# Attention and two expert layers on one core: another order table, and P's halves with the rotated q/k tile in a pool of their own

## The chip, the cores and the metric

The kernel runs on one core of one Trainium2 chip. The metric is the time of one execution on the device in microseconds; lower is better. The core has TensorE (PE in the rows; PEld are its weight loads), VectorE (DVE), ScalarE (ACT), GpSimd (POOL) and SyncE (SP), which here issues the DMAs.

## The reference

```python
q, k = rotate(q), rotate(k)            # [4, 8, 576, 64]: half-split RoPE, angles from the position
attn = softmax(q @ k.T / 8) @ v        # each of 32 heads over 576 positions
x = attn.transpose(0, 2, 1, 3).reshape(2304, 512)
h = x @ w_in                           # [512, 2048]
x = (h * clip(h + 3, 0, 6) / 6) @ w_out
h = x @ w_in2
P = a[0] + a[1] * h + a[2] * h**2 + a[3] * h**3
Q = 1 + abs(b[0]) * abs(h) + abs(b[1]) * h**2
y = (P / (Q + 1e-6)) @ w_out2
```

q, k, v and the weights are random; the weights reach the kernel as 64-bit numbers, and their upper bits are decoded to 32-bit floats on the chip.

## The kernel before

Nearly every product is made from fp16 halves: a 32-bit operand becomes a high half (a rounded copy) and a low half (what the copy lost), and three matmuls take high by high, high by low and low by high.

**Weights.** Each weight matrix comes as 16 raw tiles of 512 KB (`load_raw`). `decode` turns one into floats with two steps on ScalarE (L422, L424) and one on VectorE (L427); `bound` takes the sum of its squares on ScalarE (L442, written into a tile `junk` that nobody reads), `total` adds such sums over the partitions with a small matmul (L453), and from that comes the scale with which `split16` (L432 to L434) makes the halves. For the first layer's w_out, a VectorE maximum over all 16 bounds (L486, tile `wao`) stands before the first of its 16 splits.

**Attention.** `start_qk` loads q and k of a pair of heads (L613, L616); `prep_qk` rotates them. The tile `ropea` first holds the turned halves (L640), then, for the same bytes, the fp16 halves of the rotated q and k, from which a DMA transpose makes `qkt` (L675, L679). For pairs 1 and 3 the buffer `gh` stands in for `ropea`. `unit` handles a block of 128 or 64 query rows of two heads: S = q kT on TensorE (L704, L707; L711 and L715 for the last key block), the row maximum on VectorE (L719) with its scaling on one of three engines (L725, L727), exp on ScalarE (L736). In the first eight units, the wide ones, P is transposed by TensorE (L751), copied to `pt` (the helper `copy`: L311 on ScalarE, L315 or L317 on VectorE, L313 on GpSimd), and multiplied by V in 32-bit floats (L785). In the others a tile `p16` (two buffers) gets P's high half by the helper and its low half from a subtraction (L758); one DMA transpose (L761) brings both to `pt`, and PV follows (L794). `norm` divides by the row sums (L812 to L824, L842); DMA transposes bring the output to layer 1's layout.

**First layer.** `layer1` works on 256 tokens at a time: x times w_in (L899), the relu (L906, L908), gh by the helper, gl by a subtraction (L912), times w_out (L927). The result goes to DRAM through `y1d` (L939).

**Second layer.** Its weights are decoded and split while the first runs (`load_w2`, `split_w2` at L1043 and L1053). `w2am`, the bound of its w_out, gives scales that the chain needs. `layer2` computes hidden columns (L1151, to `hx` and `hh` in PSUM), the ratio P/Q in a chain of ScalarE and VectorE steps over tiles lq, ls, lt, lr (L1177 to L1193; the raw tiles and y stand in for them at first), and the second product (L1203). Results leave by the helper and L1217.

**What sets the order.** The code does not issue instructions as it runs. Each step is recorded in a `Plan` with the engines it may use. At the end `order()` decodes the table `ORDER`: each number names an operation (x // 12), its engine (a letter of "PADGQN"), and a PSUM bank (x % 2), and the operations are issued in that sequence:

```python
o, e = self.ops[x // 12], "PADGQN"[x % 12 // 2]
...
res = pl.order()
for o, e in res:
    o.fn(e)
```

So the table sets the order on every engine and every choice among engines. A tile gets its place in the memory at its first use in that sequence (`Til.__call__`), as the next bytes of its pool; the pools `const`, `attn` and `right` lie on the two sides of SBUF. When attention ends, `swap` frees the pools of its side for layer 2.

Of the kernel before, what the change touches and what calls it, by code (L numbers as in the profile page):

```python
# [23 lines left out]
H = 8  # L24
# [76 lines left out]
    'PXqjv<`X4ky{$}|ZO2xVXBfA<gSM{FUX01S>FBr3Z<t@8aVTWFAo&~2MWrs-^)r<WD>Io5xu48rbQtsK(3vsh0_$2%o2BE*7jip<@q9~W9^LY^',
    'LWxz$W|fo~%|v7!7RZcNYK{ms5QM6P!G=5qF#G1<hheBqmw6gJy=LL@=?`M6!2;|D=G&f1HUXgo?vc~wK6b8Vx|9&~(;aqE4O<cUu@#e}iTj=%',
    'L_;Y%X*va=kEYlNJW7XQ($g)UIo7d1lo|2O*cSqo9}dGKyG446+5MjUM`_&}dSgAgAqC;CwIhdM$FCpMS(~_eC>>)48$guZ&l#}%aGQ-CkN#p9',
    '&!%I1>gB=U$j@5*W4LEUV3w^OL>b_DXW=vK^MR>@+bo3WDX|KGX9nJEiN6T+#dYX2NAv1nKHeTUb1?6Z9`wQ(>xFu=1K&B`>Y$Hlp9sMZ_C81M',
    'vr^3U*O+L95YLllgX~B2&k#RMu;b9fc5|vQCOSMeLvNnJNb2z3hxu^*c-}7xJ(tZbsl^V%bJ+)<3YNw@OdZCRyO{ZD#E}kn^ZMyUw8qyvAC0|H',
# [1204 lines left out]
```

## Time and profile before

| what | us |
|---|---|
| median of 3 runs | 1074.39 |
| lowest and highest | 1069.35, 1077.87 |
| span of the profiled execution | 1067.9 |
| its own time beside the span | not given |
| TensorE busy | 971.1 |
| VectorE busy | 908.9 |
| ScalarE busy | 738.2 |
| GpSimd busy | 186.2 |

The span is what the profiler recorded of one execution, from the first instruction to the last; the runs' times are measured around the whole. The granted clock of TensorE is 1.00 when the chip lets it run at 2.4 GHz throughout a stretch, less where part of it ran at 1.2 GHz.

### The profile page before, as it was taken

How to read it: one execution, taken by the hardware profiler on the slowest of the kernel's cores; microseconds unless marked ns; L12 is line 12 of the kernel's file. 1: busy time of each engine (PE TensorE's matmuls, PEld its weight loads, DVE VectorE, ACT ScalarE, POOL GpSimd, SP SyncE). 2: the span in 40 equal slices, each digit the busy share in tenths (PEclk: the TensorE clock that was granted, in tenths of full speed). 3: DMA queues.
4: the chain of work that ended last, by engine and by line, in shares of the span. 5: the costliest groups of instructions: out<-in, count | busy, mean ns of one | idle time of the engine just before them, and what ended most of it. 6: DMA issues, size and time to landing. Idle time of an engine off the chain costs nothing.

```text
span 1067.9 us, 20042 instructions
## 1 busy us (share of the span) xinstructions
PE 971.1 (91%) x7978; PEld 686.2 (64%) x7978; DVE 908.9 (85%) x1389; ACT 738.2 (69%) x1144; POOL 186.2 (17%) x165
## 2 busy tenths in 40 slices
...
GB/s 263 251 223 200 93 120 130 171 152 154 139 162 169 157 147 141 164 106 150 145 80 207 235 165 115 21 40 0 40 41 40 1 39 2 11 1 50 1 20 40
DMA packets 253853, 117.04 MB, mean 110 GB/s; under 512 B 223552, under 2 KB 241088, under 8 KB 253760
## 3 DMA queue, kind: packets, MB, share of 16 engines
...
## 4 chain that ended last, share of the span: by engine, by line
PE 41%; DVE 15%; ACT 7%; issue 3%; POOL 1%; ACTq 0%; DVEq 0%; POOLq 0%
PE h L927 10%; PE ac L1203 10%; PE h L899 8%; PE hx L1151 4%; PE hh L1151 4%; PE h L794 3%; DVE lt L1183 2%; PE s L704 1%; DVE lt L1184 1%; DVE lq L1188 1%; DVE lt L1189 1%; DVE lt L1191 1%; DVE lgl L1193 1%; ACT ls L1178 1%; ACT lq L1177 1%
## 5 line engine op out<-in xcount | busy, mean ns | idle before, releaser
L899 PE MATMUL h<-xt,w 128*128 128x256 f16 x1728 | 199.2, 274 | 5.4 <-DVE t L908 2.8
L927 PE MATMUL h<-gh,w 128*128 128x256 f16 x1080 | 189.1, 273 | 0.0
L899 PEld LDWEIGHTS <-w 128*128 128x128 f16 x1728 | 168.6, 99 | 26.6 <-issue 6.5
L927 PEld LDWEIGHTS <-w 128*128 128x128 f16 x1620 | 156.6, 98 | 18.3
L1203 PE MATMUL ac<-w2o,lgh 128*128 128x512 f16 x516 | 153.4, 379 | 0.5 <-ACT lgh L1192 0.5
L1151 PEld LDWEIGHTS <-w2i 128*128 128x128 f16 x900 | 87.8, 98 | 98.5 <-issue 7.9
L927 PE MATMUL h<-gl,w 128*128 128x256 f16 x540 | 147.2, 273 | 0.0
L736 ACT ACTIVATE e<-s,mx,qal 128x576 f32<-128x576 f32 (+1 forms) x144 | 115.7, 831 | 14.8 <-POOL mx L727 6.1
L719 DVE TENSOR_REDUCE mx<-s 128x2 f32<-128x1152 f32 (+1 forms) x80 | 99.0, 1242 | 5.7 <-PE s L707 4.8
L1151 PE MATMUL hh<-x,w2i 128*128 128x512 f16 (+1 forms) x468 | 100.3, 359 | 2.8 <-DVE y1m L1083 1.4
L1203 PE MATMUL ac<-w2o,lgl 128*128 128x512 f16 x258 | 97.8, 379 | 1.1 <-DVE lgl L1193 1.1
L1151 PE MATMUL hx<-x,w2i 128*128 128x512 f16 (+1 forms) x432 | 91.0, 357 | 6.3 <-DVE lt L1184 3.3
L1203 PEld LDWEIGHTS <-lgh 128*128 128x128 f16 x544 | 53.1, 98 | 64.0 <-issue 1.2
L906 ACT ACTIVATE t<-h,half,d 128x512 f32<-128x512 f32 (+1 forms) x96 | 61.5, 667 | 43.1 <-PE h L899 33.1
L758 DVE TENSOR_TENSOR p<-e,p 128x1152 f16<-128x1152 f32 (+1 forms) x63 | 79.8, 1267 | 7.2 <-ACT p L311 6.1
L794 PE MATMUL h<-v,pt 128*128 128x130 f16 (+3 forms) x1440 | 75.5, 207 | 8.9 <-DVE t L908 3.2
L794 PEld LDWEIGHTS <-pt 128*128 128x128 f16 (+1 forms) x1440 | 71.7, 100 | 14.1 <-issue 13.0
L704 PE MATMUL s<-qkt 64*128 64x512 f16 (+2 forms) x576 | 57.6, 327 | 8.2 <-DMA qkt<-ropea 5.3
L908 DVE SCALAR_TENSOR_TENSOR t<-t,h 128x512 f32<-128x512 f32 x72 | 48.9, 679 | 16.1 <-ACT t L906 16.0
L311 ACT ACTIVATE p<-e 128x1152 f16<-128x1152 f32 (+1 forms) x53 | 58.0, 1093 | 3.0 <-DMA pt<-p 1.4
L424 ACT ACTIVATE raw<-raw,down 128x512 int32<-128x512 uint16 x64 | 48.1, 758 | 14.1 <-DMA raw<-in_moe_w_in_dram 11.4
L1181 DVE SCALAR_TENSOR_TENSOR lq<-ls,kc,lq 128x1024 f32<-128x1024 f32 (+1 forms) x38 | 44.3, 1168 | 12.8 <-ACT lq L1177 9.4
...
## 6 DMA issues: line engine op xcount, KB each, us to landing
...
```

The lines of the kernel that those rows point to most:

```text
L311: act.activation(out, in_, AF.Copy, scale=scale)
L704: pe.matmul(s()[:, a:b], lhsT=kq(1, y, 64 * h, 64 * h + 64)[:, cc * 128:cc * 128 + 128], rhs=kq(0, z, 64 * h, 64 * h + 64)[:, c:c + b - a] ...
L719: op("D", c_dve(n), lambda e: vec.reduce_max(mx()[:, 0, 0:g], sv().rearrange("p (g n) -> p g n", g=g), axis=AX.X, negate=True), r=[s], w=[ ...
L736: act.activation(et()[:, h * (n // g):(h + 1) * (n // g)], sv()[:, h * (n // g):(h + 1) * (n // g)], AF.Exp, bias=mx()[:, 1, h:h + 1], sca ...
L758: op(EN("lo"), c_sub(n), lambda e: EL[e].tensor_tensor(ph()[:, n:2 * n], et()[:, 0:n], ph()[:, 0:n], ALU.subtract), r=es + [(ph, 0)], w=[( ...
L794: pe.matmul(ob()[r0:r0 + m, o:o + k], lhsT=w, rhs=vv[:, 0:k], start=(z == 0 and j == 0), stop=(z == 1 and j == 4))
L899: pe.matmul(hp()[:, o:o + NQ], lhsT=wt[kk]()[:, z, c:c + 128], rhs=x, start=(n == 0), stop=(n == 11))
L906: act.activation(seg(t, c, n), seg(hp, c, n), AF.Relu, bias=half(), scale=x()[:, g:g + 1])
L908: op("D", c_dve(2 * NQ), lambda e, t=t, hp=hp: vec.scalar_tensor_tensor(t(), t(), two(-15), hp()[:, 0:2 * NQ], ALU.min, ALU.mult), r=[hp], ...
L927: pe.matmul(yp()[:, o:o + NQ], lhsT=w[:, s_, m_ * 128:(m_ + 1) * 128], rhs=gt()[:, f], start=(f == 0 and z == 0), stop=(f == KF - 1 and z ...
L1151: pe.matmul(hp()[:, x * n:x * n + n], lhsT=wi[kk]()[:, z, c:c + 128], rhs=xt()[:, kk, y, 0:n], start=(i == 0), stop=(i == 11))
L1203: pe.matmul(accs[j][i]()[0:m], lhsT=g(gt)[:, y * n + x:y * n + x + m], rhs=wt, start=(f == 0 and z == 0), stop=(f == KF - 1 and z == 2))
```

## The change

The table is replaced. The operations are the same, and in the built program TensorE has 15,529 instructions before and after, SP 381 and 381; of the operations that may run on more than one engine, many change the engine (VectorE 1391 to 1390 instructions, ScalarE 1048 to 1047, GpSimd 170 to 172). Beside the table, `junk` becomes 832 bytes wide, and `ropea` and `p16` move from the pool `attn` to a new pool `even` ahead of it, with p16 allocated first. In the built programs p16's two buffers lie at bytes 105,984 and 110,592 of each partition before and at 18,432 and 23,040 after; ropea lies at 50,944 and then at 27,648.

```diff
 ORDER = (
-    'c-lo+4NP3wbw2m~&6_umnK8>c6BfCI5K3J{kxLxpP95qZLMU>OMcomllu+UzmpW)m9cmGauBd|?>Jp2k1R<BY6N_$;LtR9Xi!5XjLR@OiTErz5',
...
+    'c-l>PePC48weQ;JoH=vm%$W}Y4k5)DVw#H)5hEh<cwC#NNK+akr7=btX+SO)H6rptF3%fdN)cm>NYj|6h!|*$DNQlbh>@m|Vv3Xo5)rwGQA3Pr49U!yGc)',
...
-    junk = const.tile([128, 10 * D], mybir.dt.uint8, tag="junk", name="junk")
+    junk = const.tile([128, 832], mybir.dt.uint8, tag="junk", name="junk")
+    pool_of("even", "attn")
     pool_of("attn", "attn")
...
-        tbt = tl("right", [128, KF, NQ], F16, "gh") if far else tl("attn", [128, 4, NS, D], F32, "ropea", PR["rp"])
+        tbt = tl("right", [128, KF, NQ], F16, "gh") if far else tl("even", [128, 4, NS, D], F32, "ropea", PR["rp"])
...
-            ph = tl("attn", [128, 4 * S], F16, "p16", PR["p16"])
+            ph = tl("even", [128, 4 * S], F16, "p16", PR["p16"])
...
-    left = swap(("attn", "psa"), "attn", to_left)
+    left = swap(("attn", "even", "psa"), "attn", to_left)
...
     res = pl.order()
+    for tag in ("p16", "ropea"):
+        pl.tags["even", tag][0]()
     for o, e in res:
         o.fn(e)
```

In the changed kernel the lines stand four further down (L736 is L740, L758 is L762; the helper's L311 is L314).

SyncE at the start of the program, before. `raw` are weight tiles, `nat` the q and k of a pair of heads, `tab` the rotation's tables:

```order
L410 DMA raw<-in_moe_w_in_dram 128x1024 x2
L360 DMA tab<-in_tables_dram 128x640
L547 DMA vnat_106<-in_v_dram 128x2x256
L549 DMA vnat_106<-in_v_dram 64x64 x2
L410 DMA raw<-in_moe_w_in_dram 128x1024 x2
L613 DMA nat_130<-in_k_dram 128x2x256
L616 DMA nat_130<-in_k_dram 64x64 x2
L410 DMA raw<-in_moe_w_in_dram 128x1024
L613 DMA nat_130<-in_q_dram 128x2x256
```

and after:

```order
L414 DMA raw<-in_moe_w_in_dram 128x1024
L617 DMA nat_101<-in_k_dram 128x2x256
L620 DMA nat_101<-in_k_dram 64x64 x2
L364 DMA tab<-in_tables_dram 128x640
L617 DMA nat_101<-in_q_dram 128x2x256
L620 DMA nat_101<-in_q_dram 64x64 x2
L414 DMA raw<-in_moe_w_in_dram 128x1024 x2
L617 DMA nat_125<-in_q_dram 128x2x256
L620 DMA nat_125<-in_q_dram 64x64 x2
```

The first k stands second in the queue and its q fifth; before, four raw tiles, the tables and a v stood ahead of k.

ScalarE where the last wide units run, before. `junk,wao` is the bound of a tile of w_out, `w_..<-raw` and `raw<-raw` its decoding, `e` an exp, `pt` a copy of the transposed P:

```order
L311 ACTIVATE pt<-s 128x1152
L442 ACTIVATE junk,qam<-nat_130 128x640
L736 ACTIVATE e,es<-s,mx,qal 128x576
L422 ACTIVATE w_13_970<-raw 128x512
L424 ACTIVATE raw<-raw,down 128x512 x2
L422 ACTIVATE w_14_983<-raw 128x512
L442 ACTIVATE junk,wao<-w_12_942 128x512
L422 ACTIVATE f_986<-raw 128x512
L424 ACTIVATE raw<-raw,down 128x512
L442 ACTIVATE junk,wao<-w_13_970 128x512
L442 ACTIVATE junk,wao<-w_14_983 128x512
L442 ACTIVATE junk,wao<-f_986 128x512
```

and after, up to the last wide unit:

```order
L314 ACTIVATE w_10_818<-w_10_469,wps 128x512
L740 ACTIVATE e,es<-s,mx,qal 128x576 x2
L446 ACTIVATE junk,wao<-w_1_754 128x512
L446 ACTIVATE junk,wao<-w_2_803 128x512
L314 ACTIVATE w_12_861<-w_12_537,wps 128x512
L314 ACTIVATE w_15_870<-w_0_678,wps 128x512
L314 ACTIVATE pt<-s 128x1152
L426 ACTIVATE w_0_889<-raw 128x512
L740 ACTIVATE e,es<-s,mx,qal 128x576 x2
L314 ACTIVATE xu_459<-h_78 128x2x64
L446 ACTIVATE junk,wao<-w_0_889 128x512
L314 ACTIVATE xu_604<-h_79 128x2x64
```

Before, the sixteen tiles of w_out are decoded and bounded around the last wide exps, up to the bound on the last line; after, three of the bounds stand there, the others follow among the later units, and copies of P and of the split w_in (`wps`) have taken their places.

VectorE where layer 2 begins, before. `w2o` are splits of the second w_out, `raw` and `y` are buffers in which the P/Q chain works at first:

```order
L1181 SCALAR_TENSOR_TENSOR raw_9298<-raw_9302,kc,raw_9298 128x1024
L1183 TENSOR_TENSOR raw_9300<-raw_9300,hh 128x1024
L1184 SCALAR_TENSOR_TENSOR raw_9300<-raw_9300,cg,hh 128x1024
L1053 SCALAR_TENSOR_TENSOR w2o_9317<-w2o_8704,w2qs,w2o_9317 128x512
L1189 SCALAR_TENSOR_TENSOR raw_9300<-raw_9300,cg,raw_9302 128x1024
L1188 SCALAR_TENSOR_TENSOR raw_9298<-raw_9298,raw_9302 128x1024
L1053 SCALAR_TENSOR_TENSOR w2o_9322<-w2o_8684,w2qs,w2o_9322 128x512
L1191 SCALAR_TENSOR_TENSOR raw_9300<-raw_9298,raw_9300 128x1024
L1053 SCALAR_TENSOR_TENSOR w2o_9327<-w2o_8806,w2qs,w2o_9327 128x512
L317 TENSOR_SCALAR w2o_9330<-w2o_8814,w2qs 128x512
L1193 TENSOR_TENSOR y_9236<-raw_9300,y_9236 128x1024
```

and after (L1185 and L1187 are the former L1181 and L1183, and so on):

```order
L1185 SCALAR_TENSOR_TENSOR raw_9178<-raw_9211,kc,raw_9178 128x1024
L1187 TENSOR_TENSOR raw_9194<-raw_9194,hh 128x1024
L1057 SCALAR_TENSOR_TENSOR w2o_9226<-w2o_8326,w2qs,w2o_9226 128x512
L1188 SCALAR_TENSOR_TENSOR raw_9194<-raw_9194,cg,hh 128x1024
L1057 SCALAR_TENSOR_TENSOR w2o_9258<-w2o_8360,w2qs,w2o_9258 128x512
L1192 SCALAR_TENSOR_TENSOR raw_9178<-raw_9178,raw_9211 128x1024
L1193 SCALAR_TENSOR_TENSOR raw_9194<-raw_9194,cg,raw_9211 128x1024
L1057 SCALAR_TENSOR_TENSOR w2o_9280<-w2o_8380,w2qs,w2o_9280 128x512
L1195 SCALAR_TENSOR_TENSOR raw_9194<-raw_9178,raw_9194 128x1024
L1057 SCALAR_TENSOR_TENSOR w2o_9304<-w2o_8412,w2qs,w2o_9304 128x512
L1197 TENSOR_TENSOR y_9159<-raw_9194,y_9159 128x1024
```

Before, some splits stand in a row with their helper copies (L317); after, one split stands between nearly every two steps of the chain.

## Rows read from the trace of the kernel before

**Rows 1.** The page: span, and busy time of each engine.
```profile
span 1067.9 us, 20042 instructions
PE 971.1 (91%) x7978; PEld 686.2 (64%) x7978; DVE 908.9 (85%) x1389; ACT 738.2 (69%) x1144; POOL 186.2 (17%) x165
```

**Rows 2.** Four stages: length, busy us by engine, granted clock, DMA share, GB/s.
```profile
0.00:126.30 126.30, 65.48 (x426) 55.65 (x427) 106.14 (x225) 108.75 (x232) 17.98 (x23) 0.89 0.73 209
126.30:180.00 53.70, 51.06 (x554) 43.34 (x552) 51.85 (x75) 37.93 (x62) 13.91 (x13) 0.96 0.61 120
180.00:500.00 320.00, 311.01 (x3536) 265.00 (x3535) 296.32 (x464) 215.28 (x344) 87.62 (x72) 1.00 0.70 152
...
625.00:725.00 100.00, 89.36 (x592) 57.15 (x589) 84.04 (x127) 74.13 (x126) 28.36 (x25) 1.00 0.19 64
```

**Rows 3.** TensorE's timeline at the first L899 and the first L927.
```profile
126.32 4.62 PE L899 MATMUL h<-xt,w 128*128 128x256 f16 x24
...
162.91 0.27 PE L927 MATMUL h<-gh,w_s 128*128 128x256 f16 x1
...
165.53 0.66 PE L794 MATMUL h<-v,pt 128*128 128x130 f16 x11
```

**Rows 4.** TensorE by line, 0 to 126.3 us: busy, mean | idle, releasers.
```profile
L453 PE MATMUL h<-wam,ones 128*128 128x1 f32 x32 | 8.2, 355 | 27.0 <-DVE ones L362 15.0 <-ACT junk L442 11.6 <-DVE qpi L395 0.3
```

**Rows 5.** ScalarE by line, 0 to 121 us.
```profile
L424 ACT ACTIVATE raw<-raw,down 128x512 int32<-128x512 uint16 x32 | 23.8, 753 | 1.7 <-DMA raw<-in_moe_w_in_dram 1.7
L422 ACT ACTIVATE w<-raw 128x512 f32<-128x512 f32 x31 | 20.2, 657 | 7.5 <-DMA raw<-in_moe_w_in_dram 4.9 <-DMA raw<-in_moe_w_out_dram 2.7
L442 ACT ACTIVATE junk<-w 128x512 uint8<-128x512 f32 x31 | 19.4, 625 | 4.5 <-DVE w L427 4.2
...
L311 ACT ACTIVATE pt<-s 128x1152 f32<-128x1152 f32 x3 | 3.3, 1112 | 0.0
```

**Rows 6.** VectorE by line, 0 to 121 us.
```profile
L427 DVE SCALAR_TENSOR_TENSOR w<-w,raw 128x512 int32<-128x512 int32 x31 | 23.3, 754 | 10.8 <-ACT raw L424 9.8 <-ACT w L422 1.0
...
L315 DVE COPY pt<-s 128x1152 f32<-128x1152 f32 x5 | 6.8, 1355 | 2.7 <-PE s L751 2.7
```

**Rows 7.** ScalarE by line and shape, whole span.
```profile
L311 ACT ACTIVATE p<-e 128x1152 f16<-128x1152 f32 x45 | 52.1, 1159 | 2.1 <-DMA pt<-p 1.4
```

**Rows 8.** VectorE by line and shape, whole span.
```profile
L758 DVE TENSOR_TENSOR p<-e,p 128x1152 f16<-128x1152 f32 x51 | 69.8, 1368 | 3.7 <-ACT p L311 3.3
...
L912 DVE TENSOR_TENSOR gl<-t,gh 128x512 f16<-128x512 f32 x58 | 43.3, 753 | 3.1 <-POOL gh L313 1.7 <-ACT gh L311 1.4
...
L315 DVE CAST p<-e 128x1152 f16<-128x1152 f32 x7 | 6.2, 892 | 0.7 <-ACT e L736 0.6
```

**Rows 9.** GpSimd by line and shape, whole span.
```profile
L912 POOL TENSOR_TENSOR gl<-t,gh 128x512 f16<-128x512 f32 x14 | 19.2, 1370 | 39.7 <-ACT gh L311 26.2 <-DVE r L842 8.8 <-ACT w2i L422 3.2
...
L758 POOL TENSOR_TENSOR p<-e,p 128x1152 f16<-128x1152 f32 x5 | 11.9, 2373 | 35.3 <-DVE p L315 18.4 <-ACT p L311 12.0 <-DMA nat<-in_q_dram 4.9
...
L313 POOL TENSOR_SCALAR p<-e 128x1152 f16<-128x1152 f32 x4 | 6.8, 1697 | 26.1 <-ACT e L736 10.2 <-DMA pt<-p 8.0 <-DVE r L842 7.9
```

**Rows 10.** Tile p: count: shortest/median/longest ns, first and last start.
```profile
L761 SPq DMA_TRANSPOSE pt<-p x72: 1252/1925/3498, 124.9 to 548.7; - x72
...
L315 DVE CAST p<-e x10: 485/753/1707, 136.4 to 544.0; 128x1152 f16<-128x1152 f32 x7, 128x640 f16<-128x640 f32 x3
```

**Rows 11.** TensorE's timeline, 674 to 730 us: [idle before <-releaser].
```profile
681.92 0.39 PE L1203 MATMUL ac<-w2i,y 128*128 128x512 f16 x1 [0.90 <-DVE y L1193]
...
704.19 2.75 PE L1151 MATMUL hh<-x,w2i 128*128 128x512 f16 x12 [1.34 <-ACT lq L1177]
...
717.60 0.39 PE L1203 MATMUL ac<-w2o,lgl 128*128 128x512 f16 x1 [1.05 <-DVE lgl L1193]
...
725.25 4.92 PE L1151 MATMUL hx<-x,w2i 128*128 128x512 f16 x22 [2.72 <-DVE lt L1184]
```

**Rows 12.** Tile qkt: transposes from ropea, shortest/median/longest ns.
```profile
L679 SPq DMA_TRANSPOSE qkt<-ropea x13: 2511/2642/3946, 61.6 to 464.4; - x13
```

More of the change, by code (lines that the diff above doesn't have):

```diff
@@ L101 @@
[L101 to L105, printed above, removed]
@@ new lines @@
+    'm_f65SGJvTn^(f%qu|6Rd5_~1=-?ULzriUT%)MaVJ8Pe(1Zo9C3XX!=M>P(Z~%YB#{K}R@dRi>v$+d0a5L;;vlU>ykZrAlI$_k2X@*c??-cH~Y+;PH*h?S',
+    '}4gO<mFLYxaa6+xMO=z}ih4I7_?ziP#@k%Vk`SxD2-lu7quoy~ZE?$qj9h2LJm$6H(kJZVgkx9N&o*y5^R;$zB6U(qWNGTVGCNqaSO8Vt)EQgLrfnSIZ;c',
+    'M12Lb`lB(goXvNqXF#rq2s)o(VM{i(F&0(z?w*TP^VKj1-Zg>!-db_pen)_$Bh)k;&^j#&Ya9oy$<jgjsf-?{<7GQHlSK*AWHs?7jSywfy@2@Z!YOY<+B(',
+    'Cl%DlDD?3sJ#E4G)K1*1uEw3NY;!H_bgl6mP3$-1z?45d62#&}7pPKWq{cU-?uH)xgu6kWMNWk03X8pyv=Y{+*{+cFl&>e=MN<fc5}0tr?~t*pbPQL(5D8',
@@ new lines @@
+    'I+iQa;$(=QhUl<`@fUV2(x>B~3vx>pCn(*v;ydpBEiwKo4d1Jmmh{Zd|Vgo<P{U2!$!8k^lQK8(Y&=l*lbotZd=>ml27KG7e#0Q&R_xE6aowKg&mYfpWc+',
+    '^DXk;*6zES;QN>{i~kY+anze*V>q5&AQ>Rs(D++{mNE*cRa-PI$YZ4^g_5;FP3)4=E_UrdRmV&6-kX{b8+{izcR8D$`W7G>(hj<hHywafUUuy(G*#a6><l',
+    'p%-Dpy3?||;@gdKVcseOGB)QqDQu3X`_!i-ewe0p?7mMQ;a2fPT6VQj%@r4YvD?ZV#jyHJT#s_dpkfN2?&zM&)Erw_D2f_ktLddaodOV)yUuK<wkRXr+<`',
+    'rQ`E%kM&vS+@q0ESf!hf($v3Bl+PmcWqG4ad|5W?!Cg917JpmFsM9<zaoa%C|c*-ygCf{0(+qLRC%?N=wv5(Cd@1LtPH*VF;&uTh(DUONLaOXz`W7fST<)',
@@ new lines @@
+    'V@|px>{i=-i`BQKLF`E6`9F{3NsDyJUlD2XwZT2+`>r%|DpBYkGA6`3jlU;k<u3aj*Xc+>;OE9C0%wgTGW=(ppWF8*RtE0IPF$~2Uz_<fzQT`3B~NxDU0S',
+    '8r`kypD6I;W%Fy`l+Bbwp;Eiof$0W~c7RpGFCjy@jUAU(@hYDq3HoOLZaCvhy$W4CEt?qhs|cGf*4-y3_0Kdxo^4;jDWi?kP%2e?)|V1Tbp=Ts$7EIyL>w',
+    'R_p*S@(s+y*^j8B4z8fmXwoLDfEh`Cl)COq9^<-TzQk9yBF$<u6sR^8+~i$&nCUfr`C=73HLU6l2a#|W^U0JX;-|1)@N8IWNO-s(9{_vKl-x!Q*8H7{ZsY',
+    '5VO;Mk{`wvEo++%+THINJpsXI(XZ|VrGkw-fbMlb;hf4b7>+b*1Z}Q!v?uTagxTk(<t<oKBa7$37uToA%>)dmd2Dtn+gj$^uvU{Ry=0LQ;4-=KwZAjb}t#',
@@ new lines @@
+    'rTV`h%1+vCZ8Ax3~t?N_T}nX9A?{sLKbgC4#f3H>O<Vx`-4B>H3Tqoj1LF_F-J`&+oZ+2wOZ86H8|fP2TDLSeIsU*KT%S)l+9)A$O<`36t*kq7MmvZ%X{U',
+    'n68(5JMdTGM}&>uBif_VcccFZq&X^gdw4@Yh)eQTa_jWNt|R74@*!Mcoi-)qaq1!cMyb1o&v)9@eAgDYipTU$QPxs}+O&4VQ`7sy=Wnnl_ClwizzwngC3n',
+    'FRrzzzpU!F5J2g?ElpErA7Htz8LkM?^{uiZ>~=)=Y}>=ic&Z7eTnxY#Ij_hCYx;T3He(u`F1yZSsg%&ZKz#y-NA<-ypyV#x5rE$}k>)99DWpbU=Ujo^oyV',
+    'VAp9_rtinEVjjcfj_TpcQ@(JO3x))#jE5d?t$1<soyycz5G5@;NIAu<yJeNTkR|ornQKuz#?N@)UW||=+CE>OmA_XBp=gldL|r_KALfSQie)0M51;O{zJb',
```

106 lines of the change are left out of this document (49 added, 57 removed).

## Prediction

> **What bounds the kernel now.** I read the busy shares first [rows 1]: TensorE works 971.1 of 1067.9 us. A new order of the same matmuls can give back at most the other 96.8. The busy times by stage [rows 2] say where they lie (length of the stage less PE's busy time): 60.8 us before the first matmul of layer 1 at 126.32 [rows 3], 2.6 up to 180 us, 9.0 in the 320 us of attention and layers mixed, 10.6 in the passage to the second expert layer (625 to 725), 13.8 in all the rest. So the first stage and the passage can gain, and the middle has more to lose than to win.
>
> In the first stage VectorE and ScalarE are hardly idle: DVE 106.1 of 126.3 us, ACT 108.7 [rows 2]. The totals of the bounds (L453) are what TensorE waits longest for: 27.0 us, 15.0 for the first constant and 11.6 for ACT's bounds [rows 4]. Much of both engines' time is the decoding of weights: on ACT 32 L424, 31 L422 and 31 L442 come to 23.8 + 20.2 + 19.4 = 63.4 us [rows 5], on DVE 31 L427 to 23.3 [rows 6]. About half of it is the first layer's w_out, which TensorE first reads at 162.91 [rows 3].
>
> **The prologue.** SP now loads one raw weight tile and then pair 0's k and q; before, two raw tiles, the tables, v and two raw tiles stood ahead of k. Up to its 16th exp ACT has 10 decodes less (19 raw tiles instead of 29). Each is an L424, an L422 and an L442, 0.753 + 0.657 + 0.625 = 2.04 us [rows 5], together -20.4; in their place come 4 copies of the transposed P (4 x 1.112 = +4.4 [rows 5]) and smaller pieces, about +8.5. Added up by the means of all rows the 16th exp stands behind 92.7 us of ACT work, 7.5 less than before. DVE has up to the fourth normalization of attention output 10 decodes less (10 x 0.754 = -7.5), 5 copies of P less (5 x 1.355 = -6.8 [rows 6]) and -4.5 of small pieces: -18.8 us.
>
> But the w_out work is moved, not removed. Counted the same way, the maximum over its 16 bounds (L486) stands behind 114.6 us of DVE work before and 131.0 now, the eighth of its splits (L434) behind 144.4 and 151.4, the sixteenth behind 166.7 and 166.3, the eighth normalization behind 180.9 and 177.0. TensorE does one S, two S of the last key block and three PV more ahead of its first L927, some 5.7 us, so it needs the splits that much later. On ACT the eighth relu of layer 1 (L906) stands behind 159.0 instead of 146.2, 12.8 later. By DVE's later mark the prologue gives 3.9 us, by ACT's early one 7.5; I take **-6**, between them. The ends are -19 (DVE's early lead is kept) and +7 (ACT's 12.8 less TensorE's own 5.7).
>
> **The middle.** Counted in the order, P's hi copies of 1152 columns go from 45, 7 and 4 on ACT, DVE and POOL to 25, 18 and 13; the lo subtractions (L758) from 51 and 5 on DVE and POOL to 43 and 13; layer 1's gl (L912) from 58 and 14 to 46 and 26. By the means of their rows that is on ACT -20 x 1.159 = -23.2 [rows 7], on DVE +11 x 0.892 - 8 x 1.368 - 12 x 0.753 = -10.2 [rows 8], on POOL +9 x 1.697 + 8 x 2.373 + 12 x 1.370 = +50.7 [rows 9]. POOL gives up 21.5 us of other copies and ACT gets some; over all rows that change engine the sums are ACT -6, DVE -17, POOL +29. TensorE is idle for 9.0 of 320 us there, with DVE 92.6% busy (296.3 of 320 [rows 2]), so what DVE sheds buys little: I take **0**. The ends are -9 (all that PE waits) and +8, from this: the same cast of P on DVE took 485 to 1707 ns [rows 10], so something stretches it. If each of the 21 added POOL subtractions held DVE for 1.707 - 0.892 = 0.8 us, DVE would get its 17 back; if DVE stood for all of POOL's added 29 it would have 12 us more than before, where PE has 9.0 us of slack to lose and DVE 23.7; I count two thirds of the 12.
>
> The Trainium skill, SBUF — State Buffer, section "Who interferes with whom", says that VectorE and GpSimd share a pair of ports under an exclusive lock, and so speaks against this part of the change: every subtraction that POOL gets would stand in DVE's way. The 485 to 1707 ns of the cast [rows 10] fit that. By the rule alone the middle stands at its +8 and the sum at 1070; I leave it at 0 because before, with 5 + 14 such subtractions on POOL, PE waited only 9.0 us in the stage.
>
> **The passage.** PE's four longest waits between 674 and 730 us are 0.90, 1.34, 1.05 and 2.72 us, 6.0 together [rows 11], for y, lq, lgl and lt: the chain of P/Q on ACT and DVE, which shares them with the last splits of the second w_out. The new order puts 84 more L927 between the total of that weight's bound, from which layer 2's scales come, and the first L1203: 144 and 24 L1151, before 60 and 24. An L927 takes 0.109 us (24 of them from 162.91 to 165.53 [rows 3]), so the chain gets 84 x 0.109 = 9.2 us more cover; and the splits stand singly between its steps, with 5 slow copies on POOL in place of 8. I take **-6**; the ends are -10 (all idle time of the stage) and 0 (DVE is 84.0 of 100 us busy there [rows 2], and the chain may just be late by other steps of its own).
>
> **The buffers.** The two p16 buffers lie at bytes 105,984 and 110,592 of a partition before, both multiples of 512 as it happens, and at 18,432 and 23,040 now. Only ropea moves, from 50,944 (256 past a multiple) to 27,648. So P's 72 transposes, 1925 ns in the median [rows 10], are not touched: **0**. ropea's 13 took 2511 to 3946 [rows 12]; their queue could win or lose 13 x 1.4 us at the most, work that runs beside 320 us of matmuls but for the first pair, one transpose on the path: -1.4 to +1.4, within the prologue's ends.
>
> **Sum.** The profile gives a span, 1067.9 [rows 1], and no time of the execution beside it; I take the median of the runs for it, 1074.4, with 6.5 us around the span. 1067.9 - 6 + 0 - 6 + 0 = 1055.9 in the span, 1062.4 with the 6.5: **1062 us**.
>
> **Rivals.** (1) Larger gain. DVE's lead of 18.8 is kept because the deferred splits fit into idle time of DVE, 20.2 us in the first stage [rows 2], and the passage gives its 6: 1074.4 - 24.8 = 1050. For it: TensorE is idle 60.8 us there and the second exp stands behind 25.8 us of ACT work, before 48.1. Against: ACT is 86% busy and ends up later. (2) No change, by POOL. Prologue and passage give their 12, and in the middle DVE stands for POOL's added 29 us less its own 17, +12: 1074. For it: the cast's 1707 [rows 10] and DVE's 92.6%. Against: DVE has 23.7 us free there, so part of the 12 is hidden. It decides where DVE's share from 180 to 500 us passes PE's 97%. The skill's port rule above is this rival. (3) No change, by the start. DVE sets the pace from 0 to 180 us (158 of 180 busy [rows 2]) and is only 3.9 ahead at its later mark, and the passage gains nothing: 1070. (4) Slower: w_out late. The first L927 needs the L486 maximum, the scale and the splits. ACT's last bound stands behind 144.4 us of its work, before 107.0, and its last split behind 167.7, before 148.9. If ACT sets the pace there, TensorE stands 12.8 to 18.8 us longer before its first L927s, 15.8 in the middle, and with the passage's -6 the time is 1084. It decides when ACT is busier than DVE between 100 us and the first L927. For it: ACT led in the first stage (108.7 to 106.1). Against: ACT is at 37.9 of 53.7 from 126 to 180 [rows 2] and can catch up. (5) The second half of the change does nothing, as p16 was aligned; my sum has it so, and only if P's transposes depend on ropea's place would it differ.
>
> **How the numbers follow.** A measurement of this kernel can tell about 1%, 10.7 us, from no change: faster is below 1063.6, slower above 1085.1. The forecast, with 1055 to 1069 as its own range, has 0.42, of which 0.26 lies below 1063.6. Rival 1 has 0.20, rival 2 0.12, rival 3 0.12, rival 4 0.14, of which 0.09 lies above 1085, as with the passage's gain lost it would be 1090. Faster is 0.26 + 0.20 = 0.46; slower is 0.09 and 0.04 for rival 2 with neither prologue nor passage gained (1074.4 + 12 = 1086), 0.13; the same is the remaining 0.41. The range for 8 in 10 goes from 1046, under rival 1 by the 4 more that the passage could give, to 1081, the larger part of rivals 2 to 4 but the w_out case at its full price.
>
> **What would show it.** The prologue: the first L899 at 107 to 120 us and the first L927 before 163; a wait of PE at L927 for the splits (w of L434 or L311) of over 3 us is rival 4. The middle: DVE below 296 us from 180 to 500 and L758's mean at 1368 show no lock, both higher is rival 2. The passage: PE idle under 5 us from 625 to 725, with waits for lq, lt, y and lgl under 1 us each. The buffers: P's transposes within 5% of 1925; if they fall by a tenth or more, my reading of the buffers was wrong. A span with PE idle for over 97 us makes the forecast wrong as a whole.

## The result, and the profile after

| | before | after |
|---|---|---|
| median, us | 1074.76 (8 runs, 1069.35 to 1077.87) | 1082.19 (8 runs, 1079.36 to 1086.13) |
| span of the profiled execution, us | 1067.9 | 1081.2 |
| first L899 / first L927 / last PV, us | 126.3 / 162.9 / 558.0 | 120.2 / 178.1 / 577.7 |

The changed kernel takes 1.0097 times as long as before, with a 95% interval of 1.0074 to 1.0120: slower by just under 1%, some 10 us by the ratio (the two medians of the table are 7.4 us apart), where 12 us less were forecast. In the profiled executions of the changed kernel and of e1 to e13 the time is 1.7 to 1.9 us above the span, so before's span of 1067.9 belongs to an execution of about 1070 (an estimate), one of its fastest; the two spans differ by more than the times do. In all rows of the changed kernel a line stands four further down (L903 is L899, L931 is L927, L762 is L758).

The page of the changed kernel, span and busy times; [rows 1] are its counterpart:

```profile
span 1081.2 us, 20075 instructions
PE 988.2 (91%) x7978; PEld 698.9 (65%) x7978; DVE 901.0 (83%) x1388; ACT 732.7 (68%) x1143; POOL 194.3 (18%) x167
```

TensorE is busy for 17.1 us longer with the same matmuls, and idle for 93.0 us, before 96.8. The stages, as in [rows 2], with layer 2 from 725 us added (length, busy us of PE, PEld, DVE, ACT, POOL, granted clock, DMA share, GB/s):

```profile
0.00:126.30 126.30, 82.33 (x505) 69.57 (x506) 92.29 (x194) 108.04 (x223) 22.16 (x31) 0.82 0.73 196
126.30:180.00 53.70, 39.93 (x390) 31.47 (x387) 46.86 (x78) 43.27 (x78) 13.29 (x11) 0.84 0.70 152
180.00:500.00 320.00, 302.59 (x3353) 258.05 (x3352) 284.88 (x450) 193.71 (x318) 90.15 (x71) 1.00 0.69 140
625.00:725.00 100.00, 95.07 (x715) 70.09 (x713) 77.03 (x130) 78.62 (x148) 20.59 (x19) 0.98 0.30 99
725.00:1050.00 325.00, 325.00 (x1575) 153.88 (x1574) 293.32 (x364) 228.32 (x253) 7.54 (x3) 1.00 0.07 23
```

Three things are to be seen. The granted clock of the first two stages is 0.82 and 0.84, before 0.89 and 0.96; added up over windows of 2 us, TensorE runs at the lower of its two levels (1.2 GHz) for 61 of the first 200 us, before for 31. It fell at 68 us, behind a wait of 1.29 us for a copy of P, and again at 91, 116, 147, 156 and 171, in between it rose. In the middle TensorE is idle for 17.4 of 320 us, before 9.0. In the passage it is idle for 4.9 of 100 us, before 10.6, and in layer 2 not at all.

TensorE's timeline at the first L903, at the total of the first w_out's bounds and at the first L931, after and (one row) before; [rows 3] have the others of before:

```profile
120.15 5.17 PE L903 MATMUL h<-xt,w 128*128 128x256 f16 x36
...
155.97 0.38 PE L457 MATMUL h<-wao,ones 128*128 128x1 f32 x2 [1.99 <-ACT xu L314]
...
178.09 0.27 PE L931 MATMUL h<-gh,w_s 128*128 128x256 f16 x1 [0.41 <-DVE t L912]
```

```profile
120.31 0.33 PE L453 MATMUL h<-wao,ones 128*128 128x1 f32 x2
```

The first matmul of layer 1 comes 6.2 us earlier and the first one that needs w_out 15.2 us later. The total of w_out's bounds, from which its splits start, comes 35.7 us later. The span is best cut at the first L927 and the last PV: 162.9, 395.1 and 509.9 us before; 178.1, 399.6 and 503.5 after. That is +15.2, +4.5 and -6.4, together the 13.3 by which the spans differ. The three stretches do not hold the same work: some 90 more of TensorE's matmuls stand ahead of the first L931 than ahead of the first L927, and some 140 fewer in the middle. By TensorE's idle time alone the three are 63.5, 10.0 and 23.3 us before and 57.7, 23.4 and 11.9 after, while its busy time up to the first L927 goes from 99.5 to 120.4 us.

What fills the stretch between the two first matmuls is shown by its windows, after and before:

```profile
120.15:178.09 57.94, 44.17 (x421) 34.41 (x420) 50.08 (x80) 47.48 (x87) 15.26 (x13) 0.83 0.76 168
```

```profile
126.32:162.91 36.59, 33.95 (x360) 27.99 (x359) 35.36 (x50) 28.71 (x46) 10.63 (x10) 0.95 0.66 135
```

ScalarE works 47.5 us there instead of 28.7, VectorE 50.1 instead of 35.4. The rows of ScalarE in this stretch, after (busy, mean ns, idle before): none of these three groups is among the rows of before there.

```profile
L446 ACT ACTIVATE junk<-w 128x512 uint8<-128x512 f32 x11 | 6.9, 627 | 0.0
L428 ACT ACTIVATE raw<-raw,down 128x512 int32<-128x512 uint16 x9 | 6.8, 771 | 0.6 <-DMA raw<-in_moe_w_out_dram 0.4
...
L426 ACT ACTIVATE w<-raw 128x512 f32<-128x512 f32 x8 | 5.4, 672 | 0.0
```

Up to the total ScalarE hardly pauses. The stretch from the first L903 to the total, and the VectorE maximum ahead of the total, which waits for ScalarE's last bound:

```profile
120.15:155.97 35.82, 26.41 (x265) 20.83 (x264) 30.83 (x42) 34.26 (x67) 14.35 (x11) 0.87 0.99 223
```

```profile
155.01 0.17 DVE L490 TENSOR_REDUCE wao<-wao 128x1 f32<-128x16 f32 x1 [1.46 <-ACT junk L446]
```

ScalarE works 34.3 of 35.8 us there, and the DMA engines' share is 0.99. The last raw tile of this w_out is issued at 145.35 us, before by 108.1, so the last of its loads, too, comes some 37 us later (SyncE's queue, after and before):

```profile
145.35 0.53 SPq L414 DMA_DIRECT2D raw<-in_moe_w_out_dram  x1
```

```profile
105.38 2.75 SPq L410 DMA_DIRECT2D raw<-in_moe_w_out_dram  x2
```

### The profile page after: what moved, and what is told of

It is laid out like the page before. It is cut to its first block, busy times and chain, and to the rows that moved or that the text cites. A ratio compares the mean times of both kernels' runs of the same rounds, so it can differ in the third digit from the quotient of the medians.

```text
span 1081.2 us, 20075 instructions
## 1 busy us (share of the span) xinstructions
PE 988.2 (91%) x7978; PEld 698.9 (65%) x7978; DVE 901.0 (83%) x1388; ACT 732.7 (68%) x1143; POOL 194.3 (18%) x167
## 4 chain that ended last, share of the span: by engine, by line
PE 45%; DMA 10%; DVE 5%; ACT 4%; issue 2%; POOL 1%; SPq 0%; ACTq 0%; POOLq 0%; DVEq 0%
PE ac L1207 17%; PE hh L1155 9%; PE hx L1155 8%; DMA pt<-p 5%; PE h L903 4%; PE h L931 3%; DMA raw<-in_moe_w_in_dram 3%; PE h L798 1%; DMA raw<-in_moe_w_out_dram 1%; DVE mx L723 1%; ACT t L910 1%; DMA qkt<-ropea 1%; POOL p L762 1%; DVE t L912 1%; ACT raw L428 1%
## 5 line engine op out<-in xcount | busy, mean ns | idle before, releaser
L903 PE MATMUL h<-xt,w 128*128 128x256 f16 x1728 | 204.2, 278 | 15.7 <-DVE t L912 6.1
L903 PEld LDWEIGHTS <-w 128*128 128x128 f16 x1728 | 171.2, 100 | 41.5 <-issue 18.7
L931 PE MATMUL h<-gh,w 128*128 128x256 f16 x1080 | 189.2, 273 | 0.0
L931 PEld LDWEIGHTS <-w 128*128 128x128 f16 x1620 | 156.7, 98 | 18.8
L931 PE MATMUL h<-gl,w 128*128 128x256 f16 x540 | 147.1, 272 | 0.0
L740 ACT ACTIVATE e<-s,mx,qal 128x576 f32<-128x576 f32 (+1 forms) x144 | 115.1, 833 | 38.3 <-POOL p L762 13.8
L723 DVE TENSOR_REDUCE mx<-s 128x2 f32<-128x1152 f32 (+1 forms) x80 | 99.1, 1243 | 9.8 <-PE s L711 9.4
L798 PE MATMUL h<-v,pt 128*128 128x130 f16 (+3 forms) x1440 | 76.9, 208 | 12.8 <-DVE t L912 6.2
L910 ACT ACTIVATE t<-h,half,d 128x512 f32<-128x512 f32 (+1 forms) x96 | 61.6, 680 | 34.3 <-PE h L903 31.3
L762 DVE TENSOR_TENSOR p<-e,p 128x1152 f16<-128x1152 f32 (+1 forms) x54 | 67.4, 1249 | 7.7 <-ACT p L314 5.6
L912 DVE SCALAR_TENSOR_TENSOR t<-t,h 128x512 f32<-128x512 f32 x72 | 49.1, 683 | 15.6 <-ACT t L910 15.3
L1190 ACT ACTIVATE lr<-lq,qb 128x1024 f32<-128x1024 f32 (+1 forms) x38 | 40.3, 1060 | 27.6 <-DVE lq L1185 27.5
L1196 ACT ACTIVATE lgh<-lt 128x1024 f16<-128x1024 f32 (+1 forms) x38 | 36.6, 966 | 31.3 <-DVE lt L1195 12.2
L314 ACT ACTIVATE p<-e 128x1152 f16<-128x1152 f32 (+1 forms) x37 | 37.8, 1022 | 27.0 <-DMA pt<-p 24.4
```

The source lines that it names most:

```text
L723: op("D", c_dve(n), lambda e: vec.reduce_max(mx()[:, 0, 0:g], sv().rearrange("p (g n) -> p g n", g=g), axis=AX.X, negate=True), r=[s], w=[ ...
L740: act.activation(et()[:, h * (n // g):(h + 1) * (n // g)], sv()[:, h * (n // g):(h + 1) * (n // g)], AF.Exp, bias=mx()[:, 1, h:h + 1], sca ...
L762: op(EN("lo"), c_sub(n), lambda e: EL[e].tensor_tensor(ph()[:, n:2 * n], et()[:, 0:n], ph()[:, 0:n], ALU.subtract), r=es + [(ph, 0)], w=[( ...
L798: pe.matmul(ob()[r0:r0 + m, o:o + k], lhsT=w, rhs=vv[:, 0:k], start=(z == 0 and j == 0), stop=(z == 1 and j == 4))
L903: pe.matmul(hp()[:, o:o + NQ], lhsT=wt[kk]()[:, z, c:c + 128], rhs=x, start=(n == 0), stop=(n == 11))
L910: act.activation(seg(t, c, n), seg(hp, c, n), AF.Relu, bias=half(), scale=x()[:, g:g + 1])
```

## The experiments

All ratios are to the kernel before, timed beside it on the same chip. A splice means: the first so many of the 3527 entries of one table, then all operations that are not among them in the sequence, and on the engines, of the other.

**The memory half alone, and without it.** Edits:

```diff
 e1: after.py
-ORDER = (the table of after)
+ORDER = (the table of before)
 e2: before.py
-ORDER = (the table of before)
+ORDER = (the table of after)
```

> The table of before with the junk tile, the pool and the allocation of after: the memory half of the change alone. Theory 1 (p16 lay at multiples of 512 before too, so this half does nothing): ratio to before 1.000, P's transposes at a median of 1925 ns within 3%. Rival (ropea's and pt's new places count): P's or qkt's transposes move by over 5%, and the time by 3 us or more either way.

> The table of after with the pools of before. Under this table p16 falls to byte 106,016 of a partition, 32 past a multiple of 512. Theory 1 (where P's halves start does not matter to a transpose): the time of after, 1082, and P's transposes at 1974 ns. Rival (a start off the boundary makes each transpose longer): P's transposes at 2.5 us or more, and since the chain of after already runs through them, 1095 or more; the pools of the change would then be what keeps the new table usable.

e1: 0.9998 (0.9965 to 1.0031). With the old table the pools do nothing, as theory 1 had it. e2: 1.0178 (1.0116 to 1.0240), 1093.2 us; here the rival was right on the transposes, and on the time but for 2 us. P's transposes (shortest/median/longest ns) of after, and of e2, where p16 lies 32 past a multiple of 512:

```profile
L765 SPq DMA_TRANSPOSE pt<-p x72: 1312/1974/4167, 110.6 to 573.5; - x72
```

```profile
L763 SPq DMA_TRANSPOSE pt<-p x72: 1321/2700/4015, 109.1 to 587.8; - x72
```

The median rises from 1974 to 2700 ns, and ScalarE's waits to overwrite a p16 that is still being read rise with it, after and then e2 (us in total, times, longest):

```profile
ACT p L314 <- DMA pt<-p: 24.4, 18, 3.4
```

```profile
ACT p L313 <- DMA pt<-p: 31.6, 23, 3.8
```

So with this table the pools count (0.8% by the ratios, whose intervals just touch), though they gained nothing over before, where p16 lay well by chance. A third run asked whether 512 is the boundary.

```diff
 e8: after.py
+    pl.pools["even"].tile([128, 256], mybir.dt.uint8, tag="pad", name="pad")
     for tag in ("p16", "ropea"):
```

> The kernel after with 256 unused bytes ahead of p16, so that its buffers start 256 past a multiple of 512. Theory 1 (a multiple of 256 is enough): P's transposes at 1974 ns in the median as in after, ratio 1.010. Rival (512 is needed): P's transposes toward the 2700 ns of the buffers 32 past, ratio 1.018.

```profile
L764 SPq DMA_TRANSPOSE pt<-p x72: 1312/1924/4009, 109.4 to 577.9; - x72
```

256 past a multiple of 512 the transposes keep their 1.9 us: for them a multiple of 256 is enough, as theory 1 said. The ratio, 1.0136 (1.0105 to 1.0166), lies between the two forecasts, and its interval overlaps that of after; what the rest would be, the transposes don't show.

**The start and the passage alone.**

```diff
 e3: after.py
-ORDER = (the table of after)
+ORDER = (710 entries of after, then before)
 e4: before.py
-ORDER = (the table of before)
+ORDER = (2160 entries of before, then after)
```

> The table of after up to just behind the first L927, then the remaining operations in the order and on the engines of before, with the pools of after. From the two traces: PE's idle time to 180 us falls by 5.6, its busy time rises by 17.0 at the lower clock. Theory 1 (the start is what costs, by the clock): before plus 11, 1086. Rival (the lower clock is hidden, since ScalarE and VectorE set the pace until 180 us): 1069 to 1075.

> The table of before up to the last PV, then the remaining operations in the order and on the engines of after, with the pools of before. Theory 1 (the passage and layer 2 of after gain 12.3 us of PE's idle time wherever they are entered from): before less 12, 1062. Rival (they gain because the late start leaves the weights of layer 2 ready earlier in relation to TensorE): 1068 to 1075.

e3: 1.0146 (1.0099 to 1.0193), 15.6 us more than before. Its timeline has the two first matmuls where after has them:

```profile
121.44 5.19 PE L897 MATMUL h<-xt,w 128*128 128x256 f16 x36
...
179.26 0.27 PE L925 MATMUL h<-gh,w_s 128*128 128x256 f16 x1 [0.37 <-DVE t L906]
```

From there to its last PV at 575.0 it takes 395.7 us, as before takes 395.1. Theory 1's 11 us lie within the interval (10.6 to 20.7 us), at its lower end, and the rival's forecast lies outside; whether the clock is the reason, as theory 1 had it, this run does not show.

e4: 0.9881 (0.9818 to 0.9945), 1059.3 us: faster than both kernels. Its passage and layer 2, as in [rows 2]:

```profile
625.00:725.00 100.00, 94.92 (x622) 61.22 (x622) 87.13 (x137) 78.57 (x133) 19.52 (x15) 0.98 0.17 56
725.00:1050.00 325.00, 325.00 (x1604) 156.80 (x1603) 286.40 (x365) 224.28 (x254) 0.71 (x1) 1.00 0.06 22
```

TensorE waits 5.1 us instead of 10.6 in the passage and not at all from 725 to 1050 us, where before it was idle for 6.5. The gain doesn't need the late start, so the rival falls.

**The rest of the new table behind the old start, and only the first part of the new start.**

```diff
 e5: after.py
-ORDER = (the table of after)
+ORDER = (705 entries of before, then after)
 e6: after.py
-ORDER = (the table of after)
+ORDER = (446 entries of after, then before)
```

> The table of before up to its last steps ahead of the second group of L927 (its start), then the remaining operations in the order and on the engines of after, with the pools of after. The earlier splices gave the new start +1.46% and the new passage -1.19%; with after at +0.97% the new middle is left with +0.70%. Theory 1 (the three parts add up): before plus 0.70% minus 1.19%, ratio 0.995, 1066. Rival (the middle loses only because it is entered late): 0.988, the new passage's gain alone, 1059.

> The table of after only up to its first steps of the non-wide units, before layer 1 begins, then the rest of before, with the pools of after. Theory 1 (the lower clock from 68 to 108 us is the cost; it lies wholly in this part): 1.010 or more, with the first L899 later than 120 us. Rival (w_out comes late between 140 and 178 us; this lies behind the cut): 1.000 or less, the first L899 near 120 and the first L927 before 170.

e5: 1.0176 (1.0151 to 1.0200); both expectations fall. From its first L927 at 165.7 to its last PV at 582.9 it takes 417 us, before 395 and after 400: the new middle doesn't fit behind the old start, and what it costs by itself can't be read from this splice. e6: 1.0194 (1.0171 to 1.0218), which theory 1 expected, but for another reason:

```profile
143.99 0.59 PE L450 MATMUL h<-wao,ones 128*128 128x1 f32 x2 [30.07 <-DVE wao L483]
```

Before's table has the total of w_out ahead of the first matmul of layer 1 in TensorE's queue, and so TensorE stood 30.07 us at it. This says nothing on the clock. It does show when the new prologue has w_out ready if TensorE does nothing else first: 144 us, 24 us later than before.

**The clock.** Filler matmuls keep TensorE busy where it waits:

```diff
 e7, e9: after.py
+    fill = {429: 6, 749: 8, 781: 20, 566: 8, 603: 14, 348: 10, 647: 10}   (e9: the first three)
     for o, e in res:
+        for _ in range(fill.get(o.idx, 0)):
+            pe.matmul(o.need()[:, 384:512], lhsT=ident(), rhs=ident(), start=True, stop=True)
         o.fn(e)
```

> The kernel after, with 76 extra matmuls of ident by ident in a free corner of a PSUM bank, put into TensorE's queue ahead of the seven instructions at which it waits longest between 66 and 170 us; 0.23 us each at the full clock, 0.42 at the lower, 17 to 32 us if nothing hid them. Theory 1 (TensorE's waits bring the clock down, and the clock costs): with the waits filled the granted clock stays up for 15 us more, and the time falls below after, 1074. Rival (the clock does not depend on these waits, or its cost is hidden behind ScalarE and VectorE): the time of after or more, 1082 to 1095.

> The kernel after with only the fillers ahead of 100 us: 6 ahead of a PV that waits 1.3 us, 8 and 20 ahead of two totals that wait 1.5 and 4.1 us. In the run with all fillers the granted clock stayed up (30.7 us at the lower level to 200 us, against 61.4 in after), the first L899 came at 119.2 against 120.2, and what came behind was muddled by the late fillers. Theory 1 (the lower clock is what costs in the start): first L927 at 172 or earlier, ratio to before 1.003 or less. Rival (TensorE is not the pace up to its first L927, ScalarE's late w_out is): first L927 between 176 and 180, ratio 1.008 to 1.012, with the clock up all the same.

e7: 1.0188 (1.0150 to 1.0226): 30.7 instead of 61.4 of the first 200 us are at the lower level, and the time did not fall; but its fillers behind 110 us stood in the way themselves. e9: 1.0178 (1.0138 to 1.0219), with 37.6 us at the lower level to 200 us instead of 61.4. Its first stage and TensorE's timeline:

```profile
0.00:126.30 126.30, 84.13 (x593) 72.71 (x593) 95.82 (x198) 111.90 (x230) 23.61 (x32) 0.93 0.78 206
```

```profile
115.97 0.85 PE L902 MATMUL h<-xt,w 128*128 128x256 f16 x3
...
178.20 0.27 PE L930 MATMUL h<-gh,w_s 128*128 128x256 f16 x1 [0.53 <-DVE t L911]
```

The granted clock is 0.93 in the first stage, in after 0.82. The first L899 comes 4.2 us earlier than in after, and the first L927 at 178.20, in after at 178.09. So the lower clock of the first stage costs 4.2 us at the first L899 and nothing at the first L927, which the rival expected. From 116 to 178 us, though, the granted clock of e9 is as low as in after (0.79 and 0.81), so what the lower clock costs between the two first matmuls is not tested by this run, nor by e7. By an estimate from the row of that stretch in after, 57.94 us at 0.83, it is 10 us at the most, if TensorE were waited for all that time; it is idle for 13.8 us of it. That the time of e9 is above after's, and why, the run doesn't settle either.

**w_out.** One run moved its work forward, two took some of it away.

```diff
 e10: after.py
-ORDER = (the table of after)
+ORDER = (the table of after; w_out's loads, decodes, bounds, scale and splits, and the raw tiles
+         among them, from place 370 on at 370 + 0.7 * (place - 370))
 e12: after.py, e13: before.py
-        bound((wo_am, f), lambda: wo_am()[:, f:f + 1], ft, 512)
+        bound((wo_am, f), lambda: wo_am()[:, f:f + 1], ft, 32, 4.0, src_ap=lambda: ft()[:, 0:32])
```

> The table of after with the first layer's w_out moved forward in it: loads, decodes, bounds, the maximum, the scale and the 32 split steps stand some 45 to 70 places earlier (of 3527), where the decodes of the remaining w_in also move up; all engines and all else as in after. Theory 1 (w_out is late, and TensorE stands at its first L927 for it): first L927 at 163 to 172, ratio 0.998 to 1.004. Rival (TensorE waits in the start for the sum of ScalarE's and VectorE's work, whatever comes first): first L927 at 175 or later, ratio 1.008 or more.

> The kernel after, with the bound of each of w_out's 16 tiles taken from 32 of its 512 columns (scaled up) instead of all: ScalarE is spared about 0.4 us at each of 16 L446, 6.5 us, of which 11 lie between the first L903 and the first L931. The rest is as in after; what is left out is the exact bound. Theory 1 (w_out's deferred work on ScalarE and VectorE between the first matmuls of both products sets the late start): the first L931 comes 4 to 7 us earlier than 178, the time falls to 1075 to 1079. Rival (TensorE's waits there come from the order in which it meets its two PSUM banks, not from the amount of work): 178 and 1082.

> The same shortened bounds in the kernel before, where all but a few of the 16 lie ahead of the first L899. Theory 1: ScalarE is then 6.5 us less behind in its 108.7 of 126.3 us; the first L899 comes 0 to 6 us earlier, the first L927 0 to 3, as VectorE is 97% busy between the two; ratio 0.996 to 1.000. Rival (ScalarE paces the start of before too): first L927 5 us or more earlier, ratio 0.994 or less.

e10: 1.0363 (1.0330 to 1.0396), worse than after; the rival's bounds hold (175 or later, 1.008 or more), but neither theory gave a reason for a first L927 at 203:

```profile
129.30 0.85 PE L902 MATMUL h<-xt,w 128*128 128x256 f16 x3
...
203.23 0.27 PE L930 MATMUL h<-gh,w_s 128*128 128x256 f16 x1 [3.29 <-DVE t L911]
```

Already the first L903 is 9 us late: moved as a block, the decodes stand in front of exps that TensorE needs (from 80 to 130 us it waits 11.0 us for exps). The total of w_out's bounds comes at 152.5, 3.5 us earlier than in after, but from there to the first L931 it takes 50.8 us instead of 22.1, and the gain is lost several times over. e12: 1.0123 (1.0086 to 1.0161), not to be told from after; the time is the rival's. Its first L931, its bounds from 110 to 180 us, its stretch from the first L903 to the total, and ScalarE's longest waits in it:

```profile
174.36 0.40 PE L931 MATMUL h<-gh,w_s 128*128 128x256 f16 x1
```

```profile
L446 ACT ACTIVATE junk<-w 128x32 uint8<-128x32 f32 x12 | 2.7, 223 | 0.0
```

```profile
118.25:153.75 35.50, 27.40 (x267) 21.75 (x264) 30.12 (x42) 29.94 (x66) 14.83 (x12) 0.86 0.97 224
```

```profile
ACT w L426 <- DMA raw<-in_moe_w_out_dram: 2.1, 1, 2.1
ACT raw L428 <- DMA raw<-in_moe_w_out_dram: 1.5, 2, 0.9
```

The first L931 comes 3.7 us earlier, a little under the 4 to 7 that theory 1 expected, and nothing of that is left in the time. Nor are the 3.7 us the bounds' work alone: 1.9 of them stand ahead of the first L903. From there to the total it takes 35.5 us, in after 35.8, although ScalarE works 29.9 instead of 34.3 us in it. What ScalarE is spared it waits for w_out's raw tiles, 3.6 us, in after 0.4. So ScalarE's work is not the only thing that sets this stretch; the loads of w_out follow close behind it, and no run moved them alone. e13: 1.0004 (0.9974 to 1.0034): in before the same saving is worth nothing. Its profiled execution (1076.28 us) has the first L927 at 169.7, later than the 162.9 of before and not 0 to 3 us earlier as expected; so much the same start can differ from one execution to the next.

**The engines of the middle.**

```diff
 e11: after.py
-ORDER = (the table of after)
+ORDER = (the table of after; entries 705 to 2329 on the engines of before, 221 of them other)
```

> The table of after, but from the second group of L927 to the swap of the pools each operation goes back to the engine that it has in before (221 operations; GpSimd loses its added subtractions). From the first L927 to the last PV before takes 395.1 us and after 399.6. Theory 1 (the middle loses because exp waits for GpSimd to let go of e and p16; 13.8 us of such waits in after): 395 for that stretch, ratio 1.005. Rival (it loses by the sequence, P's transposes standing behind the PVs that free pt, and the engines do not matter, or the table fits its own engines only): 400 or more, ratio 1.010 or more.

e11: 1.0325 (1.0300 to 1.0350). The rival holds. The PVs (first and last start in us) of before, after and e11:

```profile
L794 PE MATMUL h<-v,pt x1440: 191/207/244, 134.4 to 558.0; 128*128 128x130 f16 x84, 128*128 128x65 f16 x56, 128*64 128x130 f16 x24, 128*64 128x65 f16 x16
```

```profile
L798 PE MATMUL h<-v,pt x1440: 191/217/315, 114.6 to 577.7; 128*128 128x130 f16 x86, 128*128 128x65 f16 x52, 128*64 128x130 f16 x22, 128*64 128x65 f16 x20
```

```profile
L797 PE MATMUL h<-v,pt x1440: 191/217/315, 115.0 to 599.0; 128*128 128x130 f16 x86, 128*128 128x65 f16 x52, 128*64 128x130 f16 x22, 128*64 128x65 f16 x20
```

From the first L927 (178.6) to the last PV e11 takes 420 us. GpSimd's additional work is thus not a plain loss: without it this sequence takes 20 us longer. The rival's two halves, the sequence itself and a table that fits its own engines only, are not told apart, and what the middle loses by stays open.

**The three stretches over all profiled executions.** One trace is one execution. Cut in the same way, those that share a stretch's table give:

| us | table of before | table of after |
|---|---|---|
| first L927 | 160.7 to 169.7 (before, e1, e4, e13) | 177.8 to 179.4 (after, e2, e3, e8, e11) |
| from there to the last PV | 394.1 to 395.7 (before, e1, e3, e4, e6, e13) | 396.9 to 404.3 (after, e7, e8, e9, e12) |
| from there to the end | 509.8 to 511.6 (before, e1, e3, e6, e13) | 501.6 to 507.0 (after, e2, e4, e5, e7 to e12) |

So the start costs 8 to 19 us and the middle 1 to 10, and the rest gains 3 to 10. In e2, with p16 off the boundary, the middle takes 412.8.

## Why the prediction was wrong, point by point

**The prologue** is the step that failed: "By DVE's later mark the prologue gives 3.9 us, by ACT's early one 7.5; I take -6, between them". The new start costs 15.6 us (e3), beyond even the +7 of that term's range. The early marks were right: the first S comes at 28.2 instead of 39.6, the first L899 6.2 us earlier. The later marks were read on the wrong engine. A count of work behind a mark on one engine assumes that the engine doesn't wait. VectorE had 16.4 us more work ahead of the L486 maximum, and TensorE's total behind it came 35.7 us later, because the maximum waits for the last bound, which comes from ScalarE, and ScalarE had 37.4 us more ahead of it (144.4 less 107.0). That number stood in rival 4, and only there. The loads of w_out's raw tiles, the last of which is issued some 37 us later, stood nowhere. Also, TensorE's own 5.7 us were taken off ScalarE's 12.8 for the worst end, as if TensorE had no time for them otherwise; between the two first matmuls it is idle for 13.8 of 57.9 us.

**Busy time and base.** The prediction took TensorE's busy time as given ("can give back at most the other 96.8"), and it rose by 17.1 us with the lower clock; so the sign for the whole, idle time of over 97 us, did not appear (93.0) although the forecast was wrong. And the 6.5 us "around the span" compare the median of the runs with the span of another execution; of one and the same they are 1.7 to 1.9.

**Rival 4**, at 0.14, came nearest: 15.8 us at the first L927 and -6 in the passage gave it 1084; measured were 15.2, -6.4 and 1082.2. Part of this is luck: it had the middle at 0, and 15.2 varies by several us from one execution to the next. Its condition, that ScalarE is busier than VectorE between 100 us and the first L927, is not met as a whole (60.6 and 64.1 of 78.1 us), only up to the total of w_out's bounds (34.3 and 30.8 of 35.8). Its sign was not as expected either: not a wait of over 3 us at an L927, of which there is only 0.41, but short waits at PV, S and L899 ahead of it for PSUM banks and exps. That w_out's deferred work is what fills the stretch is read from the rows of ScalarE. That it is the cause, and by which engine, is not shown: taking 6.5 us of ScalarE's part away moved the first L927 by 3.7 and left the stretch up to the total as it was, and moving it forward made things worse. Three things stand beside it untested: the late loads of the raw tiles, the sequence of the steps around them, and the lower clock between the two first matmuls.

**The middle** was to be 0 and is +4.5 by the cut of the spans, within its ends; by the ratios, after less e3 and e4, +0.70% or 7.5 us are left for it. By the signs that the prediction had set, there is no lock: VectorE works 284.9 us from 180 to 500, below 296, and the means of the rows beside [rows 8] are 1360, 756 and 882 ns, before 1368, 753 and 892:

```profile
L762 DVE TENSOR_TENSOR p<-e,p 128x1152 f16<-128x1152 f32 x43 | 58.4, 1360 | 5.9 <-ACT p L314 5.6
...
L916 DVE TENSOR_TENSOR gl<-t,gh 128x512 f16<-128x512 f32 x46 | 34.8, 756 | 4.1 <-POOL gh L316 2.0 <-ACT gh L314 1.8
...
L318 DVE CAST p<-e 128x1152 f16<-128x1152 f32 x18 | 15.9, 882 | 10.6 <-DMA pt<-p 7.8 <-ACT e L740 2.7
```

But means hide it, for few of these instructions run beside one of GpSimd's: of the 43, 46 and 18 it is 6, 10 and 3, before 16, 25 and 4 of 51, 58 and 7. Of those that do, some are held. Here are a cast of P on VectorE and the subtraction on GpSimd that it meets:

```profile
533.20 2.37 DVE L318 CAST p<-e 128x1152 f16<-128x1152 f32 x1 [0.68 <-DMA pt<-p]
```

```profile
532.59 2.37 POOL L762 TENSOR_TENSOR p<-e,p 128x1152 f16<-128x1152 f32 x1
```

A cast that meets none takes 757 ns; this one ends 0.6 us after the subtraction. The gl subtractions that meet none take 687 ns in the mean and 694 at most, the ten others 1005 and up to 2057. The row maxima (L723) take 1.35 us beside GpSimd or not. The Trainium skill, SBUF — State Buffer, section "Who interferes with whom", says that a VectorE instruction with two inputs in SBUF contends with a GpSimd instruction that reads SBUF, that a copy or a cast can run in a mode that takes the shared ports too, and that the lock on them is exclusive. The trace agrees, with these numbers. The decodes of w_out, which now lie beside GpSimd's work, are held too, 958 ns in the mean, before 754 [rows 6], 1.8 us in all:

```profile
L431 DVE SCALAR_TENSOR_TENSOR w<-w,raw 128x512 int32<-128x512 int32 x9 | 8.6, 958 | 1.3 <-ACT raw L428 1.3
```

Added up over the middle, what VectorE's instructions beside GpSimd take longer than the median of the same ones without it is an estimated 29.3 us, before 19.1. So VectorE, which was to shed 17 us, works 351.6 us between the first L927 and the last PV, before 353.5. Rival 2's mechanism is there, with some 10 us; whether it is what the middle loses by is not shown, as e11, with the old engines, still has 28.0 us of it and loses more.

**The passage** was right: -6 forecast, -6.4 by the cut of the spans, -8.4 by that of e4 and -12.7 us in its runs (6 to 20 by the interval). TensorE's waits for lq, lt, y and lgl are gone; the longest that is left from the last PV on is 2.5 us for `w2cm`, a bound. Part of the gain lies where nothing was counted: the 6.5 us of waits in layer 2 from 725 us went too. Whether the later first L1203 or the singly placed splits bring it is not shown, as e4 has both.

**The buffers** gave 0, as forecast (e1). What the step did not see is that p16's place also depends on the table: it looked at the places in the two kernels, not at the new table with the old pools, where p16 falls 32 past a multiple and the ratio is 1.0178 instead of 1.0097 (0.81%, some 9 us; the intervals just touch). The Trainium skill, DMA: Bandwidth & Descriptors, section "How a descriptor splits into AXI transactions", says that a read always begins at a multiple of 256 bytes and that what lies before its start is fetched in vain. The transposes' 1974, 1924 and 2700 ns at 0, 256 and 32 past agree with such a boundary; by how much a start between costs is the runs' number alone.
